# A long-convolution layer and a state-space layer in one kernel: queues in a list-scheduled order, x transposed by the DMA crossbar, and wide rotations

## The chip, the cores and the metric

One core of a Trainium2 chip. The metric is the device time of one execution in microseconds (us), as the median of several runs. Names of the engines: PE is TensorE (PEld its weight loads), DVE is VectorE, ACT is ScalarE, POOL is GpSimd, SP is SyncE, which here only issues DMA transfers; a "q" behind a name (SPq) is the engine's own instruction queue. A run is called slow when it lies over 1.5% above the fastest of its kernel; ratios use fast runs alone.

## The reference, cut to what matters

Two independent layers on 2048 x 1024 inputs in bf16, their outputs side by side.

```python
# A: k shifted (4 taps) times v, long convolution by FFT, gate by q
k_shift = sum over t of k_pad[:, t:t+S] * shift_k[:, 3-t]
kv = k_shift * v
y  = irfft(rfft(kv, 2S) * rfft(ssm_k, 2S))[:S] + kv * ssm_D
a  = q * y
# B: a diagonal complex state-space layer
Lam_bar = exp(dt * Lam);  B_bar = ((Lam_bar - 1) / Lam)[:, None] * Bmat
h_t = Lam_bar * h_{t-1} + B_bar @ x_t          # 2048 steps, 1024 complex states
b  = 2 * Re(h @ Cmat.T) + x * Dskip
out = concatenate([a, b], axis=-1)
```

Both kernels do layer A as a three-stage transform with matmuls: stage one (shift products on DVE, then matmuls, results to DRAM), stage two (load, matmul, product, halves swapped by DMA, matmul, back to DRAM) and stage three (load, matmul, product with q, store). Each stage needs all of the one before. Layer B runs in 16 chunks of 128 time steps. For each: U = B x on PE, a rotation by DVE that makes the recurrence real, two scans on DVE, a rotation back, y = C h on PE. The chunks follow one another through the scan's carry. Layer B has no dependency on layer A, so its U and y matmuls may fill whatever PE leaves free.

## The kernel before

Every chunk's x is loaded plain, transposed by PE and copied by ACT. The rotation is a list of products and sums of 1024 elements. It uses `u` as scratch, so the buffer of `u` is given back with the last operation (`state.pop`). [cuts are marked with ...]

```python
    def b_load_x(i):
        xn = xpool.tile([P, D], BF16, name="xn", bufs=3)
        dma(xn[:], x[i * T:(i + 1) * T, :])
        ...
    def b_xT(i, eng="s"):
        ...
        for dd in range(ND):
            nc.tensor.transpose(pt[:, dd, :], xn[:, dd * P:(dd + 1) * P], ident[:])
        ...
            nc.scalar.copy(xT[:], pt[:])

    def b_rot_ops(i):
        ...
        ops.append(lambda: nc.vector.tensor_mul(st["tb"][:], st["u"][:, 1, :, :], si[:]))
        ops.append(lambda: nc.vector.tensor_add(st["ta"][:], st["ta"][:], st["tb"][:]))
        ...
        ops.append(lambda: nc.vector.tensor_mul(st["u"][:, 1, :, :], st["tb"][:], eor[:]))
        def o14():
            nc.vector.tensor_add(st["h"][:, 1, :, :], st["h"][:, 1, :, :], st["u"][:, 1, :, :])
            state[("h", i)] = st["h"]
            state.pop(("u", i))
```

The order comes from a table of ticks, eight for each chunk. U of later chunks is spread over the ticks at a fixed rate, the three stages of layer A have fixed steps:

```python
    U_RATE1 = cfg.get("u_rate1", 1.5)
    U_RATE2 = cfg.get("u_rate2", 0.7)
    ...
    A1_STEP = cfg.get("a1_step", 2.0)
    A2_STEP = cfg.get("a2_step", 2)
    A3_STEP = cfg.get("a3_step", 1)
    ...
    for t_ in range(-1, NT):
        e = ev.get(t_, {})
        run(e.get("misc", []))
        run(interleave(e.get("pe_b", []), e.get("pe_a", [])))
        run(interleave(e.get("dve_b", []), e.get("dve_a", [])))
```

## Time and profile before

| | before |
|---|---|
| time, median of three runs | 434.61 us (430.33 to 434.89) |
| span of the profiled run | 431.1 us, granted clock 0.974 |
| PE / DVE / ACT busy | 380.7 / 350.7 / 303.6 us |

A busy PE is not a PE at its peak, so the tables of this document count "dense" PE work instead: the number of matmuls of each shape in a stretch times the time that one takes when they follow one another without a gap (0.056, 0.109 and 0.216 us for 128, 256 and 512 columns, the middle one an estimate from the others; the list below gives the same 128-column matmul a mean of 224 ns, since they overlap). What is missing to the length of the stretch is the loss.

The first fence is the table of busy time by stretch for the kernel before (length; then busy us and number of instructions of PE, PEld, DVE, ACT, POOL; granted clock, DMA share, GB/s):

```profile
0.00:180.00 180.00, 147.58 (x1753) 118.67 (x1754) 167.81 (x334) 143.01 (x239) 71.90 (x115) 0.96 0.74 242
180.00:431.10 251.10, 233.16 (x1964) 141.02 (x1961) 182.90 (x309) 160.56 (x292) 58.34 (x109) 0.98 0.71 234
```

From then on PE is busy 233 of 251 us; before it, 148 of 180. The second is the list by line for PE in the first 180 us (count, busy, mean ns, then idle time in front and what ended it):

```profile
L274 PE MATMUL pu<-xT,BT 128*128 128x128 bf16 x976 | 76.5, 224 | 0.5 <-ACT xT L263 0.3 <-ACT BT L605 0.2
L427 PE MATMUL psa<-acc,F1t 128*128 128x512 bf16 x64 | 24.6, 392 | 12.0 <-DVE acc L414 11.9
```

976 matmuls of U are 7.6 chunks. And 12 us of PE's idle time are spent in front of the stage-one matmul, waiting for the shift product on DVE; in this order U work that stands behind that matmul on PE is not begun meanwhile. The third is DVE's timeline:

```profile
171.24 0.67 DVE L414 TENSOR_TENSOR acc<-acc,vt 128x1024 bf16<-128x1024 bf16 x1
173.65 0.67 DVE L292 TENSOR_TENSOR ta<-u,ci 128x1024 bf16<-128x1024 bf16 x1
```

The last shift product ends at 171.9 us; the rotation of chunk 5 (the sixth, counted from 0) begins at 173.65.

### The profile page before, as it was taken

To read this page: it belongs to the slowest core of one execution; us is meant where nothing else is said; L and a number is where in the kernel's file an instruction comes from. 1 tells how busy PE (TensorE), PEld (TensorE's weight loads), DVE (VectorE), ACT (ScalarE), POOL (GpSimd) and SP (SyncE) were. 2 spreads that over 40 slices of the span, in tenths; PEclk is the share of its full clock that TensorE was granted. 3 is DMA by queue.
4 is the path that set the end of the run, shared out by engine and by line. 5 is a ranking of instruction groups with operands and counts; after the bars stand their busy time and mean duration, and the time that the engine had idled before them with its cause. 6 is when DMAs were issued, how large, how long until landed. Compare 5 with 4: busy or idle time off the path is not lost.

```text
span 431.1 us, 9757 instructions
## 1 busy us (share of the span) xinstructions
PE 380.7 (88%) x3713; PEld 259.7 (60%) x3713; DVE 350.7 (81%) x642; ACT 303.6 (70%) x531; POOL 130.2 (30%) x224
## 2 busy tenths in 40 slices
PE   2589799797987997999899999999899999997784
PEld 2578687575765875775556566566465666763331
DVE  2989999999999999936897979797959637976830
ACT  1977999787886887646678877878568783344451
POOL 4000344464654455311222232322122211012121
PEclk9979999999999899999999999999899999999989
DMA  7879987778776544397778687879666523959981
GB/s 247 285 255 309 336 289 254 265 240 249 276 235 205 167 163 159 120 334 238 229 241 263 217 247 245 265 234 295 195 217 181 165 69 135 298 176 396 403 316 73
DMA packets 41353, 102.23 MB, mean 237 GB/s; under 512 B 6621, under 2 KB 8925, under 8 KB 41306
## 3 DMA queue, kind: packets, MB, share of 16 engines
q1 hardware_dynamic: 27322, 58.60, 42.7%
q0 software_dynamic: 13984, 43.01, 28.8%
q8 instruction: 29, 0.48, 0.5%
q14 instruction: 18, 0.15, 0.1%
HBM read 59.64 MB, written 33.55 MB: 216 GB/s over the span
## 4 chain that ended last, share of the span: by engine, by line
PE 42%; DVE 28%; issue 12%; DMA 10%; ACT 5%; POOL 2%; SPq 0%; POOLq 0%; DVEq 0%; ACTq 0%
PE pu L274 13%; PE py L345 13%; DVE m L409 5%; PE psa L508 5%; DVE acc L410 4%; DMA hb<-ha 3%; PE psa L533 3%; PE psa L532 3%; DVE ta L305 2%; DVE tb L308 2%; DVE acc L414 2%; DMA out_dram<-ot 2%; POOL out_dram L88 2%; DMA bn<-in_B_C_re_dram 1%; PE pt L601 1%
## 5 line engine op out<-in xcount | busy, mean ns | idle before, releaser
L274 PE MATMUL pu<-xT,BT 128*128 128x128 bf16 x2048 | 156.1, 222 | 0.5 <-ACT xT L263 0.3
L274 PEld LDWEIGHTS <-BT 128*128 128x128 bf16 x2048 | 136.2, 100 | 33.5 <-issue 2.4
L345 PE MATMUL py<-CT,h 128*128 128x512 bf16 x512 | 140.2, 382 | 2.3 <-ACT yo L355 2.3
L345 PEld LDWEIGHTS <-h 128*128 128x128 bf16 x512 | 46.7, 98 | 45.5 <-issue 4.9
L88 POOL DMA_DIRECT2D hb<-ha x64 | 33.4, 526 | 88.9 <-ACT ha L509 85.0
L534 ACT CAST vsb<-psa 128x512 bf16<-128x512 f32 x64 | 37.0, 602 | 25.7 <-PE psa L533 24.8
L88 POOL DMA_DIRECT2D Ys_h<-ysbh x64 | 45.6, 716 | 30.8 <-ACT ysbh L475 29.4
L277 ACT CAST u<-pu 128x512 bf16<-128x512 f32 x64 | 39.4, 615 | 13.2 <-PE pu L274 13.1
L428 ACT CAST ysb<-psa 128x512 bf16<-128x512 f32 x64 | 38.5, 644 | 13.7 <-PE psa L427 13.3
L519 DVE TENSOR_TENSOR ha<-x,ha 128x1024 bf16<-128x1024 bf16 x32 | 21.9, 684 | 27.8 <-DMA hb<-ha 18.7
L475 ACT CAST ysbh<-psa 128x512 bf16<-128x512 f32 x64 | 38.7, 641 | 5.5 <-issue 2.3
L509 ACT CAST ha<-psa 128x512 bf16<-128x512 f32 x64 | 36.8, 598 | 7.3 <-PE psa L508 6.3
L509 ACT CAST x<-psa 128x512 bf16<-128x512 f32 x64 | 36.9, 593 | 7.3 <-PE psa L508 5.2
L308 DVE TENSOR_TENSOR_SCAN tb<-rtab,tb 128x1024 bf16<-128x1024 f32 x16 | 36.6, 2285 | 0.0
L305 DVE TENSOR_TENSOR_SCAN ta<-rtab,ta 128x1024 bf16<-128x1024 f32 x16 | 36.5, 2280 | 0.0
L427 PE MATMUL psa<-acc,F1t 128*128 128x512 bf16 x64 | 24.6, 392 | 12.0 <-DVE acc L414 11.9
L564 ACT CAST ot<-psa 128x512 bf16<-128x512 f32 x32 | 17.9, 589 | 24.4 <-DMA out_dram<-ot 14.8
L409 DVE TENSOR_TENSOR m<-krow,wbc 128x1024 bf16<-128x1024 bf16 x48 | 32.4, 675 | 0.0
L410 DVE TENSOR_TENSOR acc<-acc,m 128x1024 bf16<-128x1024 bf16 x48 | 32.3, 673 | 0.0
L532 PE MATMUL psa<-ha,wts 128*128 128x512 bf16 x64 | 24.5, 384 | 4.2 <-DVE ha L519 4.0
L88 POOL DMA_DIRECT2D Ys_kv<-ysb x32 | 17.8, 557 | 33.9 <-ACT ysb L428 33.9
L350 PE MATMUL py<-Dd,xT 128*128 128x128 bf16 x128 | 28.0, 219 | 0.0
(139 smaller groups left out, 628.5 us busy)
## 6 DMA issues: line engine op xcount, KB each, us to landing
Ys_kv<-ysb POOLq DMA_DIRECT2D x32, 256.0 KB, 2.9
Ys_h<-ysbh POOLq DMA_DIRECT2D x64, 128.0 KB, 3.3
l2k<-Ys_kv SPq DMA_DIRECT2D x16, 512.0 KB, 6.0
l2h<-Ys_h SPq DMA_DIRECT2D x16, 512.0 KB, 4.2
hb<-ha POOLq DMA_DIRECT2D x64, 128.0 KB, 3.7
Vs<-vsb POOLq DMA_DIRECT2D x16, 512.0 KB, 5.9
vv<-Vs SPq DMA_DIRECT2D x32, 256.0 KB, 6.6
xn<-in_B_x_dram SPq DMA_DIRECT2D x16, 256.0 KB, 4.3
```

Source lines behind the costliest of these rows:

```text
L88: return nc.gpsimd.dma_start(out_, in_)
L274: nc.tensor.matmul(pu[:, c, jl, :], BT[:, j, c, dd, :], xT[:, dd, :], start=(dd == 0), stop=(dd == ND - 1))
L277: nc.scalar.copy(u[:, :, j - 1:j + 1, :], pu[:])
L305: ops.append(lambda: nc.vector.tensor_tensor_scan(fl(st["ta"]), fl(rtab), fl(st["ta"]), 0.0, ALU.mult, ALU.add))
L308: nc.vector.tensor_tensor_scan(fl(st["tb"]), fl(rtab), fl(st["tb"]), 0.0, ALU.mult, ALU.add)
L345: nc.tensor.matmul(py[:], h[:, c, j, :], CT[:, j, c, dh * 512:(dh + 1) * 512], start=(j == 0 and c == 0), stop=(j == NJ - 1 and c == 1))
L409: ops.append(lambda jj=jj: nc.vector.tensor_mul(st["m"][:], krows[n2 - jj][:], wbc[:, jj, :]))
L410: ops.append(lambda: nc.vector.tensor_add(st["acc"][:], st["acc"][:], st["m"][:]))
L428: nc.scalar.copy(ysb[:, dh * 512:(dh + 1) * 512], pt[:])
L475: nc.scalar.copy(ysbh[:, :, n2l, :], pt[:].rearrange("p (c d) -> p c d", c=2))
L509: nc.scalar.copy(d_[:, dh * 512:(dh + 1) * 512], pt[:])
L532: nc.tensor.matmul(pt[:], wts[:, gi, 1, :], ha[:, dh * 512:(dh + 1) * 512], start=True, stop=False)
```

## The change

The intent: DVE and PE should not wait for one another. (1) Instead of tick tables, every piece of work is a task with a duration, dependencies, buffers and a priority; a small list scheduler in the kernel's source makes one fixed order of all queues from them. Parameters and phase tables have the first priority on every engine. (2) Transposes through PE use two PSUM banks. (3) Each rotation is two wide operations, a product of 4096 elements into a scratch tile and a sum of 2048. (4) x is loaded transposed by the DMA crossbar. The rewrite brings smaller changes with it: shift products and second-stage products are wide too, the first k and v loads go out on POOL's queue, and the filter taps are spread over the partitions by PE instead of by the DMA. The core of the diff (nearly the whole file is replaced; cuts marked with ...):

```diff
-    def b_load_x(i):
-        xn = xpool.tile([P, D], BF16, name="xn", bufs=3)
-        dma(xn[:], x[i * T:(i + 1) * T, :])
...
-            nc.tensor.transpose(pt[:, dd, :], xn[:, dd * P:(dd + 1) * P], ident[:])
...
+    def x_(i):
+        st["xT", i] = btile("xT", [P, ND, T])
+        nc.sync.dma_start_transpose(st["xT", i][:], x[i * T:(i + 1) * T, :])
...
-        ops.append(lambda: nc.vector.tensor_mul(st["tb"][:], st["u"][:, 1, :, :], si[:]))
-        ops.append(lambda: nc.vector.tensor_add(st["ta"][:], st["ta"][:], st["tb"][:]))
...
+    def rot_mul(i, src, Z):
+        st["m", i] = btile("mt", [P, 4, W], 1)
+        m = st["m", i][:].rearrange("p (a b) w -> p a (b w)", a=2)
+        s_ = src[:].rearrange("p b j t -> p (b j t)").unsqueeze(1).to_broadcast([P, 2, 2 * W])
+        nc.vector.tensor_mul(m, s_, win(Z))
+
+    E["r1"] = lambda i: rot_mul(i, st.pop(("u", i)), Z1)
...
-        run(interleave(e.get("pe_b", []), e.get("pe_a", [])))
-        run(interleave(e.get("dve_b", []), e.get("dve_a", [])))
...
+CFG = dict(PB=20.79, t0=31.9, lead=20.0, a1s=6.3, a1e=116.9, h_s=13.7, h_e=125.7, a2s=135.2, a2e=223.8, a3s=302.3,
+           a3e=340.0, u=5, xT=8, h=2, yo=2, ps_t=2, ps_u=2, ps_y=1, ps_a=3, kr=8, ld=5, acc=2, ysb=3, hk=3, hT=2, ysbh=2,
...
+    A(("tabA1",), "DVE", 4.1, [("dve3",)], [("u", 2), ("h", 2)], pr=-58)
...
+        A(("x", i), "SP", 1.5, acq=["xT"], pr=tu - c.get("xlead", 12.0) if i else -12, nbytes=int(256 * KB * 1.75))
+        for jp in range(4):
+            tj = tu + jp * c["PB"] / 8
+            A(("U", i, jp), "PE", 1.78, [("x", i)] + [("bc", 2 * jp + a, b) for a in (0, 1) for b in (0, 1)],
+              ["ps_u"] + (["u"] if jp == 0 else []), pr=tj, after=("U", i, jp - 1) if jp else None)
...
+    with tc.manual_schedule():
+        for t in make_plan(c).run():
+            E[t.name[0]](*t.name[1:])
```

In a task line, the first list holds what it depends on, the second the buffers that it takes, `pr` is its priority (lower is earlier). Both kernels have five buffers of `u`; the new one gives a buffer back with the first product of the rotation (`r1`).

## The prediction

> **What bounds the kernel now.** I read the page's first part, then the table of busy time by stage, the timeline and the chain of waits.
>
> ```profile
> PE 380.7 (88%) x3713; PEld 259.7 (60%) x3713; DVE 350.7 (81%) x642; ACT 303.6 (70%) x531; POOL 130.2 (30%) x224
> q1 hardware_dynamic: 27322, 58.60, 42.7%
> q0 software_dynamic: 13984, 43.01, 28.8%
> ```
>
> No engine is full over the span: TensorE (PE) is nearest, VectorE (DVE) next, the DMA engines near 72% (42.7 + 28.8). So I asked by stage. Columns: stretch, its length, busy time of each engine with instructions, granted clock, DMA share, GB/s.
>
> ```profile
> 0.00:44.00 44.00, 28.48 (x382) 25.97 (x383) 33.26 (x104) 29.53 (x47) 5.42 (x14) 0.92 0.85 276
> 44.00:180.00 136.00, 119.09 (x1375) 92.70 (x1373) 134.56 (x231) 113.49 (x193) 66.48 (x102) 0.97 0.70 231
> 180.00:390.00 210.00, 204.70 (x1840) 129.33 (x1837) 162.90 (x281) 144.50 (x262) 49.72 (x94) 0.99 0.70 222
> 390.00:431.10 41.10, 28.46 (x126) 11.68 (x124) 20.00 (x28) 16.06 (x30) 8.62 (x16) 0.94 0.76 293
> ```
>
> Four stages with different limits: a start in which no engine is full and DMA is busiest; 44 to 180 us (first stage of the convolution), where DVE is busy 134.56 of 136; 180 to 390, where PE is busy 204.70 of 210; a tail in which everything waits.
>
> A busy PE is not a PE at its peak, so I counted matmuls. The chain of waits (columns: start, length, what) shows the dense rates:
>
> ```profile
> 178.40 1.79 PE pu L274 x32
> 180.19 0.86 PE py L345 x4
> ```
>
> 32 matmuls of 128 columns in 1.79 us are 56 ns each, 4 of 512 in 0.86 us are 215. From the list by line and shape: 2688 matmuls of 128 columns (2048 for pu, 128 each for the skip term and for transposes of B, C, x and the filter) are 150 us, 896 of 512 columns are 193, 128 of 256 columns at about 109 ns (half the 512 rate plus overhead, an estimate) are 14. Dense PE work is **357 us** of 431; some 74 us are idle, slow-clock or stalled. The same count in the four stages gives about 22, 111, 201 and 25 us: losses of 22, 25, 9 and 16. That is what a better order can win; the 357 it cannot, except by removing matmuls.
>
> The tail, in the chain:
>
> ```profile
> 398.12 2.90 issue
> 401.01 0.02 POOLq L88
> 401.03 0.54 POOL out_dram L88
> 401.57 2.38 issue
> ```
>
> POOL issues an output store every 2 to 3 us; the page's slices of GB/s stand near 400 there. The third convolution stage moves 4 x 4.2 MB (two halves of Vs, q, output), and most of it runs after the scan chain has nothing left to hide it with.
>
> **What the Trainium skill says.** (1) "TensorE: Matmul & The Clock Gate", section "Wait — 56ns, not 53.3ns?": warm start-to-start is 55.6 ns at 128 columns, 215.7 at 512. The trace agrees (56 and 215), so PE cannot go faster per matmul. (2) "VectorE: DVE Perf Modes", "The perf-mode tier table": tensor_tensor on bf16 reaches 2x only, 1224 ns for 2048 elements. A wider op therefore saves a fixed cost and no element time. The timeline agrees on size: 1024-element products start every 0.60 us (0.53 of it is 1024 elements at two per cycle of 0.96 GHz). (3) "Advanced Engine Details and Errata", "X-Bar Transpose (TRN2)": transpose DMAs are as fast as regular ones; "DMA: Bandwidth & Descriptors", "Latency and other measured facts", gives 261 GB/s for a non-contiguous case. No run here shows one yet. (4) The same DMA page, "Issuing engines are not separate DMA queues": all queues share 16 engines, so moving early k and v loads to POOL's queue saves issue time, not bandwidth.
>
> **The change, part by part.**
>
> Rotations. Before, per chunk, 12 products and sums of 1024 elements, 2 scans of 2.20 us and six small carry ops. The timeline shows how well they are packed already:
>
> ```profile
> 58.01 0.67 DVE L410 TENSOR_TENSOR acc<-acc,m 128x1024 bf16<-128x1024 bf16 x1
> 58.61 0.67 DVE L328 TENSOR_TENSOR u<-tb,eor 128x1024 bf16<-128x1024 bf16 x1
> 59.21 0.67 DVE L414 TENSOR_TENSOR acc<-acc,vt 128x1024 bf16<-128x1024 bf16 x1
> ```
>
> The mean of 0.67 overlaps the next; the cost is 0.60. So a chunk is 12 x 0.60 + 4.4 + about 0.6 = 12.2 us. After: two products of 4096 (2.13 + 0.07 = 2.20 each), two sums of 2048 (1.07 + 0.07, and 0.07 because each now waits on its forerunner), scans 4.4, three small ops 0.5: about 11.7. Gain 0.5 x 16 = **8 us of DVE**, far less than the drop from 14 wide instructions to 6 suggests. Shift products: 8 x 0.60 = 4.8 before, 2.20 + 1.2 + 2 x 0.67 = 4.7 after: 1 to 2 us in all. Second-stage product: 1.14 for 1.20, 2 us over 32. Four B evacuations, the x copy and two table casts leave DVE: 4.5 us; smaller parameter ops, 3. DVE falls from 351 to about **330 us**.
>
> x by crossbar. Removes 128 PE transposes, 128 x 0.056 = 7.1 us, and on ScalarE (ACT) 15 copies of 1.06, 15.9 us. It also frees two PSUM tiles for the other transposes (the pool keeps two banks). Filter broadcast through PE adds 8 x 0.22 = 1.7. PE work becomes 357 - 7 + 2 = **352 us**. ACT: -15.9, +4 B copies, +4.3 table copies, about +1 for the broadcast: 297.
>
> Order. The instruction order shows the parameter chain and tables first on each engine; all shift products done during chunks 0 to 4, second stage in chunks 5 to 13, third stage in 13 to 15, with only five q products after the last rotation. So the DMA-heavy third stage moves beside PE work, and shift products begin before the B matrices are all in.
>
> Sum by stage. DVE leads until the shift products end: about 20 us of tables and parameters + 16 x 4.7 + 5 x 11.7 = 154 us, beginning near 9 (parameters land at 7.3, and copy and Exp follow), and some 7 us of gaps: 170 us, where before needed about 180 and had DVE idle 11 us in the first 44. PE has by then done its share, some 140 us of 352 (132 before by 180). Left: 212 us of PE; at the 96% density of 180 to 390 before, 220. Then the tail: after the last rotation eight y groups (about 6.9 us of PE, part of it already in the 212), last evacuation and a store landing in 3 to 4 us, little of it hidden: +4. Span 170 + 220 + 4 = 394 at most of the old inefficiency; with the order somewhat tighter in the middle (98%), 389. The times exceed the span by 3.5 us (434.6 against 431.1). I choose **394 us**, 9% less.
>
> **Rivals.** (a) DVE becomes the bound throughout: 330 us plus a start of 9 and a tail of 11 is 350, below PE's sum, unless the stride-0 broadcast and overlapping windows of the wide products cost the 2x mode. Then 48 products of 4096 take 2.1 us longer each, +102, DVE passes 430, and the time is 440 or more. For it: no such pattern is in this trace. Against: innermost runs are dense bf16. 3%. (b) Transfers become the wait. 72% of 431 is 308 us of DMA; with slower x transposes (I add 10) and 1 MB less of broadcast, about 316 in 390, 81%; in the second stage 37 MB plus x and y in some 130 us are 300 GB/s, and the table showed 222 to 276 at shares of 0.70 to 0.85. Waits for swapped halves (18.7 us of DVE idle before) could grow: time 405 to 415. For it: a fixed order blocks a whole queue behind a late load. 20%. (c) A fixed order made from planned durations meets real ones; PE, DVE and ACT drift and stall each other as before: 410 to 425. 10%. (d) The order fits well, PE is dense from 25 us to the end: 376 to 382. 20%.
>
> **Range and chances.** The sum gives 389 to 397; (d) takes it to 378, (b) to 411. Eight in ten: 378 to 411. "Same" needs over 426, meaning all the tail's and start's gain lost: 4%. Slower only through (a) or a badly slow transpose: 2%. Faster: 94%.
>
> **What would show it.** Right: the dense count 352 us and losses of 35 to 45 instead of 74; over half of the gain in the start and tail; the last stage under 12 us behind the last rotation; DVE busy near 330 with 4096-wide products starting every 2.2 us; no x copy on ACT; second-stage DMA share above 0.8. Wrong: 4096-wide products near 4.3 us (a); x transposes landing in over 10 us or holding the SP queue, so that first pu matmuls start after 25 us (b); long waits of PE and ACT for one another with every engine under 85% (c).

## The result, and the profile after

405.76 us (403.26 to 409.58, four runs) against 433.83 (430.33 to 434.89) for the kernel before in the same rounds. A ratio here is always the mean time of one kernel's fast runs over that of the other's of the same rounds, so not quite the ratio of these medians: 0.935, 95% interval 0.928 to 0.941. Faster, by 6.5%; 12 us slower than predicted, inside the range. The profiled run took 403.26 us, with a span of 401.5. First the page's totals and the hardware DMA queue (packets, MB, share of the 16 engines' time), then the table by stretch:

```profile
PE 366.2 (91%) x3593; PEld 248.6 (62%) x3593; DVE 336.4 (84%) x338; ACT 291.6 (73%) x527; POOL 132.1 (33%) x228
q1 hardware_dynamic: 40864, 57.17, 47.3%
```

```profile
0.00:44.00 44.00, 31.06 (x382) 26.49 (x383) 30.32 (x83) 34.55 (x61) 12.15 (x26) 1.00 0.99 265
44.00:165.00 121.00, 117.08 (x1487) 95.48 (x1485) 113.02 (x98) 105.99 (x180) 59.42 (x89) 1.00 0.74 245
165.00:190.00 25.00, 19.90 (x186) 12.60 (x184) 24.34 (x21) 10.29 (x20) 3.92 (x8) 0.94 0.71 232
190.00:380.00 190.00, 183.01 (x1468) 107.28 (x1467) 159.34 (x129) 133.07 (x254) 51.70 (x97) 1.00 0.81 261
```

DVE lost 304 instructions but only 14 us. The start is no fuller than it was (PE 31 of 44 us), and there is a new hole: from 165 to 190 us, where stage two has to begin, PE is busy 19.9 of 25. The cut at 180 us, and PE's U work in the first 180:

```profile
0.00:180.00 180.00, 161.75 (x2025) 131.97 (x2025) 157.95 (x193) 148.06 (x254) 74.44 (x120) 1.00 0.79 243
180.00:401.50 221.50, 204.44 (x1569) 116.67 (x1568) 178.43 (x146) 143.55 (x273) 57.61 (x108) 0.99 0.79 259
```

```profile
L588 PE MATMUL ps_u<-xT,BT 128*128 128x128 bf16 x1280 | 79.2, 221 | 0.1
L698 PE MATMUL ps_a<-acc,F1t 128*128 128x512 bf16 x64 | 20.3, 379 | 0.6 <-DVE acc L691 0.3 <-ACT ysbh L750 0.3
```

The stretch after 180 us shrank from 251.1 to 221.5 us. Since the cut lies at the same time in both kernels, this is the whole gain of 29.6 us in span by construction. 1280 matmuls of U are exactly ten chunks, against 7.6; the wait for shift products in front of the stage-one matmul fell from 12.0 to 0.6 us. But DVE is not further on at that time:

```profile
168.27 0.69 DVE L691 TENSOR_TENSOR acc<-acc,ld 128x1024 bf16<-128x1024 bf16 x1
168.88 2.29 DVE L600 TENSOR_TENSOR mt<-u,Z 128x4096 bf16<-128x4096 bf16 x1
181.15 2.29 DVE L600 TENSOR_TENSOR mt<-u,Z 128x4096 bf16<-128x4096 bf16 x1
```

The last shift product ends at 169.0 (before: 171.9), and the rotation of chunk 5 begins at 181.15, which is 7.5 us *later* than before. So at 180 us five chunks are rotated or nearly so in both kernels (before, the sixth rotation is half done); after the change PE has U ready for five more, before for two and a half. Dense PE work by the count described above:

| | dense to 180 us | dense left | length of the rest | dense share of the rest |
|---|---|---|---|---|
| before | 132.4 | 225.6 | 251.1 | 0.90 |
| after | 152.1 | 200.5 | 221.5 | 0.91 |

Of the 25.1 us less that are left at 180 us, 5.4 are work that the change removed (358.0 us in all before, 352.6 after), 19.7 were done earlier, and 17 of these are U (304 matmuls of 0.056 us). The rest is worked off at nearly the same density, as the sum of two things that cancel in part: a better tail, and a new hole at its beginning.

Losses by stage, before: 22 (to 44 us), 25 (to 180), 9 (to 390), 16 (tail). After: 20 (to 44), 8 (to 172), 5 (172 to 190), 9 (to 380), 7 (tail from 380). Stage one with the passage to stage two gained 12 us, the tail 10, the start 2, the removed work 5.4.

One rival is the clock: the profiled runs were granted 0.974 before and 0.992 after, and within the fast runs of one kernel a lower clock goes with a longer time (0.992 and 403.26 us, 0.979 and 407.62 us for the changed kernel). It carries little of the gain. At nearly equal clocks, 0.978 for the kernel before (430.99 to 433.46 us in runs of the rounds below) and 0.979 for the changed one (407.62), 23 to 26 us remain of the 28.

What was left undone stands in the timeline of SP's queue (start, length of the issuing, what):

```profile
16.24 6.27 SPq L576 DMA_TRANSPOSE xT<-in_B_x_dram  x2
...
25.09 2.83 SPq L576 DMA_TRANSPOSE xT<-in_B_x_dram  x1
...
28.60 1.23 SPq L576 DMA_TRANSPOSE xT<-in_B_x_dram  x1
...
30.49 1.23 SPq L576 DMA_TRANSPOSE xT<-in_B_x_dram  x1
...
45.29 0.38 SPq L558 DMA_DIRECT2D ld<-in_B_B_im_dram  x1
```

Six crossbar loads of x between 16 and 32 us, three of them for chunks 5 to 7, which cannot be used before a buffer of `u` comes free at the first rotation, sit between the loads of B (issued at 24.51, 28.02, 29.93 and so on); the last B load is issued at 45.3. Every rotation needs all of B. And DVE waits for v, whose load is behind them too:

```profile
44.15 0.69 DVE L691 TENSOR_TENSOR acc<-acc,ld 128x1024 bf16<-128x1024 bf16 x1 [6.68 <-DMA ld<-in_A_v_dram]
...
56.14 2.29 DVE L600 TENSOR_TENSOR mt<-u,Z 128x4096 bf16<-128x4096 bf16 x1 [0.94 <-ACT u L590]
```

The first rotation begins at 56.14 us. Before, the first line of a rotation stood almost 19 us earlier:

```profile
37.31 0.68 DVE L292 TENSOR_TENSOR ta<-u,ci 128x1024 bf16<-128x1024 bf16 x1
```

### The profile page after: what moved, and what is told of

Its sections match the earlier page's. It is cut to its first block, busy times and chain, and to the rows that moved or that the text cites. A ratio compares the mean times of both kernels' runs of the same rounds, so it can differ in the third digit from the quotient of the medians.

```text
span 401.5 us, 9098 instructions
## 1 busy us (share of the span) xinstructions
PE 366.2 (91%) x3593; PEld 248.6 (62%) x3593; DVE 336.4 (84%) x338; ACT 291.6 (73%) x527; POOL 132.1 (33%) x228
## 4 chain that ended last, share of the span: by engine, by line
PE 42%; DMA 15%; issue 14%; DVE 13%; ACT 9%; POOL 4%; SPq 2%; POOLq 0%; ACTq 0%; DVEq 0%
PE ps_y L641 14%; PE ps_u L588 12%; PE ps_a L805 5%; PE ps_a L772 5%; DMA wts<-a_c_W 4%; DMA hab<-hab 3%; DVE h L618 3%; DMA Ys_kv<-ysb 3%; DVE hab L796 2%; DMA Ys_h<-ysbh 2%; DMA ld<-in_B_B_re_dram 2%; ACT ysbh L750 2%; POOL out_dram L850 2%; PE ps_a L698 1%; POOL Ys_h L757 1%
## 5 line engine op out<-in xcount | busy, mean ns | idle before, releaser
L641 PE MATMUL ps_y<-CT,h 128*128 128x512 bf16 x512 | 138.1, 381 | 3.6 <-ACT yo L656 1.6
L588 PE MATMUL ps_u<-xT,BT 128*128 128x128 bf16 x2048 | 126.0, 221 | 0.1
L618 DVE TENSOR_TENSOR_SCAN h<-rtab,h 128x1024 bf16<-128x1024 f32 x32 | 71.5, 2276 | 0.3
L590 ACT CAST u<-ps_u 128x512 bf16<-128x512 f32 x64 | 37.9, 604 | 41.9 <-PE ps_u L588 41.8
L796 DVE TENSOR_TENSOR hab<-x,hab 128x2048 bf16<-128x2048 bf16 x32 | 38.5, 1221 | 14.8 <-ACT hab L779 6.5
L600 DVE TENSOR_TENSOR mt<-u,Z 128x4096 bf16<-128x4096 bf16 x16 | 36.6, 2289 | 11.2 <-ACT u L590 11.0
L779 ACT CAST hab<-ps_a 128x512 bf16<-128x512 f32 x64 | 36.2, 600 | 10.8 <-DMA l2h<-Ys_h 5.7
L785 ACT CAST x<-ps_a 128x512 bf16<-128x512 f32 x64 | 36.9, 599 | 5.2 <-PE ps_a L772 5.0
L750 ACT CAST ysbh<-ps_a 128x512 bf16<-128x512 f32 x64 | 36.8, 637 | 4.3 <-DMA Ys_h<-ysbh 2.6
L600 DVE TENSOR_TENSOR mt<-h,Z 128x4096 bf16<-128x4096 bf16 x16 | 36.5, 2283 | 0.0
L553 PE MATMUL ps_t<-ident,ld 128*128 128x128 bf16 x256 | 21.1, 233 | 9.2 <-DMA ld<-in_B_B_re_dram 5.8
```

What stands on the lines that cost most here:

```text
L588: nc.tensor.matmul(pu[:, w, jl, :], BT[:, 2 * jp + jl, w, d, :], xT[:, d, :], start=(d == 0), stop=(d == ND - 1))
L590: E["ue"] = lambda i, jp: nc.scalar.copy(st["u", i][:, :, 2 * jp:2 * jp + 2, :], st.pop(("pu", i, jp))[:])
L600: nc.vector.tensor_mul(m, s_, win(Z))
L618: nc.vector.tensor_tensor_scan(gf[:, a * W:(a + 1) * W], rt1, gf[:, a * W:(a + 1) * W], 0.0, ALU.mult, ALU.add)
L641: nc.tensor.matmul(py[:], h[:, 1 - w, j, :], CT[:, j, w, dh * 512:(dh + 1) * 512], start=(j == 0 and w == 0), stop=(j == NJ - 1 and w == 1))
L750: nc.scalar.copy(st["yh", qd, n4, w // 2][:, :, w % 2, :], st.pop(("pa", qd, n4, w))[:].rearrange("p (c d) -> p c d", c=2))
```

## The experiments

All outputs are right. Before each run its author wrote down an "own theory" and at least one "rival", another explanation with another number. "Before" had medians of 433.13, 433.20, 432.44 and 432.50 us in the rounds beside these runs. Twelve kernels ran. In nine of their traces 37 to 51 of some 3600 PE records are missing, so counts and busy times of PE are a little low there; the runs with the work put back, with three chunks ahead, and the last one are complete.

### x through PE again, in the new order

The crossbar load is replaced by a plain load, eight transposes and a copy on ACT; buffers had to move for it (x 8 to 7, k rows 8 to 7), and the list was planned anew.

```diff
-        A(("x", i), "SP", 1.5, acq=["xT"], pr=tu - c.get("xlead", 12.0) if i else -12, nbytes=int(256 * KB * 1.75))
+        A(("xl", i), "SP", 1.5, acq=["xn"], pr=tu - c.get("xlead", 12.0) if i else -12, nbytes=256 * KB)
+        A(("xt", i), "PE", .45, [("xl", i)], ["ps_t", "xT"], ["xn"], pr=tu - 2 if i else -12)
+        A(("x", i), "ACT", .91, [("xt", i)], [], ["ps_t"], pr=tu - 2 if i else -12)
```

> The new kernel with x transposed on the tensor engine again (128 transposes, 16 copies on ACT; order planned anew, x buffers 7 and 2 in the same memory, key ring 7 in place of 8). My theory, dense PE work plus losses: PE work rises by 7 us, ACT by 16; most of the 7 and a little more shows: about 415 us, ratio to the kernel before 0.955. Rival A, the freed transpose banks and ACT time are the main gain: 0.975 or more. Rival B, a crossbar transpose costs the transfers what it saves the engines: 0.935, no change from the new kernel.

Measured: 424.0 us (421.87 to 426.81), ratio 0.981 (0.974 to 0.988). That looks like 18 us for the crossbar, but the trace of this kernel has one line that spoils the experiment:

```profile
55.22 0.69 DVE L702 TENSOR_TENSOR acc<-acc,ld 128x1024 bf16<-128x1024 bf16 x1 [23.39 <-DMA ld<-in_A_v_dram]
```

The new plan had put the first load of v far back, DVE stood idle for 23.39 us at once, and the first rotation moved from 56 to 72 us, which would be enough for nearly all of the 18. This run does not say what the crossbar is worth.

### The crossbar alone, in the old order

```diff
-        xn = xpool.tile([P, D], BF16, name="xn", bufs=3)
-        dma(xn[:], x[i * T:(i + 1) * T, :])
+        xT = xpool.tile([P, ND, T], BF16, name="xT", bufs=XT_BUFS + 3)
+        nc.sync.dma_start_transpose(xT[:], x[i * T:(i + 1) * T, :])
```

> The kernel before with x by crossbar DMA alone (same tick order, 10 x buffers in the memory of 7 and 3). My theory: PE work falls by 7 us, but the first stage there is bound by DVE, so only part shows: 427 to 430 us, ratio 0.985. Rival A (banks and ACT are the main gain): 0.96. Rival B (transposes as dear as they save): 1.00.

Measured: 433.92 us, ratio 1.001 (0.991 to 1.010): the number of rival B, not of the own theory. PE's busy time fell from 380.7 to 371.0 (49 of its 3585 records are missing) and ACT's from 303.6 to 288.4; the time did not move. The interval leaves room for some 4 us either way.

### The removed work put back as idle work, in the new order

Since the first of these runs was spoilt, the same question was asked in a form that leaves the new order and its loads alone: the first eight matmuls of each chunk's U done twice, and each x tile copied onto itself by ACT.

```diff
+        if jp == 0:
+            for d in range(ND):
+                nc.tensor.matmul(pu[:, 0, 0, :], BT[:, 0, 0, d, :], xT[:, d, :], start=(d == 0), stop=(d == ND - 1))
...
+        E["xc"] = lambda i: nc.scalar.copy(st["xT", i][:], st["xT", i][:])
```

> The changed kernel in its own order, with the engine work that the crossbar had removed put back as idle work: the first 8 matmuls of each chunk's U are done twice (128 matmuls of 128 columns, 7.1 us of dense TensorE work) and ScalarE copies each x tile onto itself (16 copies of 1.06 us). The loads stay on the crossbar. Own theory (from the second stage on TensorE sets the time, in the first it has slack): half of the doubled work and more lies in chunks whose U is done ahead in the first 180 us; the 6 chunks left cost 6 x 8 x 56 ns = 2.7 us, and the whole is 2 to 5 us, ratio 0.939 to 0.947. Rival one (the removed work is worth all of its 7 us): ratio 0.951 or more. Rival two (worth nothing, as in the kernel before): 0.933 to 0.937.

Measured: 409.1 us (407.36 to 410.41), ratio 0.945 (0.938 to 0.951): 3 to 4 us slower than the changed kernel, in the range of the own theory. The intervals of the two ratios overlap, so "worth a few us" is supported, "worth all of 7" is less so, and "nothing" is not excluded by much. Nor does the trace show the own theory's mechanism. The idle work delayed the start as well:

```profile
60.86 2.29 DVE L603 TENSOR_TENSOR mt<-u,Z 128x4096 bf16<-128x4096 bf16 x1 [2.27 <-ACT u L593]
```

That is the first rotation, 4.7 us later than in the changed kernel; chunk 5 follows at 188.50 instead of 181.15, and 1152 matmuls of U are done by 180 us instead of 1280. How much of the 3 to 4 us is this start, and how much is work in the full second stage, is open.

### Rotations as narrow operations, same order

```diff
-        nc.vector.tensor_mul(m, s_, win(Z))
+        for a in range(2):
+            for b in range(2):
+                nc.vector.tensor_mul(st["m", i][:, 2 * a + b, :], s_[:, b, :], z_[:, a + b, :])
```

(and the sums likewise in two of 1024)

> The new kernel with each rotation product as four products of 1024 and each sum as two of 1024, same order, same result. My theory: 12 instructions of 0.60 in place of 2 x 2.20 + 2 x 1.2 is about 0.5 us more per chunk, DVE +8 us of which a part is hidden: 408 to 411 us, ratio 0.943. Rival: the wide products are what made DVE leave the path: ratio 0.96 or more. A third, independent narrow products overlap the waits of one another: no change, 0.935.

Measured: 403.85 us (403.13 to 404.12), ratio 0.934 (0.928 to 0.940), the same as the changed kernel's 0.935 within some 3 us. DVE's timeline of this run, to be read beside the line at 168.88 us of the changed kernel above:

```profile
252.03 2.50 DVE L602 TENSOR_TENSOR mt<-u,Z 128x1024 bf16<-128x1024 bf16 x4
```

Four narrow products take 2.50 us, one wide one 2.29: 0.07 us for each operation saved (0.21 / 3). Over the kernel DVE's busy time gains 7.4 us (343.8 to 336.4) and the kernel's time nothing. From one rotation's start to the next, where DVE does nothing else, it is less: 12.27 us wide (168.88 to 181.15) and 12.57 narrow (170.42 to 182.99), since the sum behind a wide product waits for its end. Widening the operations is worth nothing here. What both kernels of this comparison keep, against the kernel before, is the scratch tile that lets `u` go after the first product.

### The third stage moved beside the last rotations, in the old order

```diff
-    A2_STEP = cfg.get("a2_step", 2)
-    A3_STEP = cfg.get("a3_step", 1)
+    A2_STEP = cfg.get("a2_step", 1.6)
+    A3_STEP = cfg.get("a3_step", 1.25)
```

> The kernel before with its second stage at 1.6 ticks a group in place of 2 and the third at 1.25 in place of 1, so the third stage lies beside the last rotations; nothing else. My theory: the tail's loss of 16 us falls to about 8, ratio 0.98 (425 us). Rival: the second stage is held by its transfers and cannot go faster, and the crowding costs PE waits there: ratio 1.00 or more.

Measured: 426.45 us (424.86 to 428.12), ratio 0.986 (0.980 to 0.993): 6.7 us, near what was expected. The trace agrees on the place: the last rotation ends at 409.65 us (410.03 before), and what follows it takes 13.5 us instead of 21.1. This is the tail's part of the gain, had in the old kernel by two numbers.

### Table part of the chain late, in the new order

```diff
-    A(("tabA1",), "DVE", 4.1, [("dve3",)], [("u", 2), ("h", 2)], pr=-58)
-    A(("eo",), "ACT", 4.8, [("sin1",), ("sin2",), ("par_rest",)], pr=-55)
+    A(("tabA1",), "DVE", 4.1, [("dve3",)], [("u", 2), ("h", 2)], pr=10)
+    A(("eo",), "ACT", 4.8, [("sin1",), ("sin2",), ("par_rest",)], pr=10)
```

(and nine more tasks of the chain in the same way)

> The changed kernel with the table part of the parameter chain (phase tables, sines, the products of Z2) no longer first: on VectorE and ScalarE the first shift products, the copies of B and of the first results stand ahead of it. Own theory: the first rotation at 56.14 us waits for results of the last B loads, not for tables, which are finished at 29.6 us; putting them 5 to 8 us later changes the start by at most 3 us, ratio 0.934 to 0.942. Rival (the table chain first is what the new order gains at the start): the first rotation moves out by 5 to 8 us and the time with it, ratio 0.947 to 0.953.

Measured: 412.42 us (411.97 to 414.26), ratio 0.953 (0.947 to 0.958). The own theory falls: it allowed 3 us, it was 6.7, the size that the rival named. The theory had looked only at when the tables are needed. DVE's waits in the first 90 us of this kernel:

```profile
DVE acc L691 <- DMA ld<-in_A_v_dram: 8.8, 2, 5.1
DVE BT L564 <- PE ps_t L553: 6.4, 3, 3.6
```

In the changed kernel the same waits are 7.2 and 4.1. The first rotation moves to 60.30 us, 4.2 later. The tables are some 13 us of DVE and 11 of ACT by the list's planned durations; put later, they stand in the queues between the copies of B, and a B load can start only when such a copy has freed its buffer. That this chain makes the 4.2 us is a reading, and the trace supports it only in part: the last B load is issued at 45.67 instead of 45.29 us, the loads of v at 41.95 and 46.93 instead of 40.03 and 45.77. In the first 44 us DVE was as busy as before (30.41 us against 30.32), and the granted clock was 0.88 instead of 1.00, which no run separates from the order.

### Loads of x for chunks 5 to 7 after the loads of B

```diff
-        A(("x", i), "SP", 1.5, acq=["xT"], pr=...
+        A(("x", i), "SP", 1.5, [("bl", 7, 1)] if 5 <= i < 8 else [("x", i - 1)] if i >= 8 else [], acq=["xT"], pr=...
```

> The changed kernel with one thing moved: the crossbar loads of x for chunks 5 to 7 go after the last load of B instead of between the B loads (and those of later chunks after them, as before). Own theory: in the changed kernel VectorE leads the first stage, and its first 56 us lose because seven crossbar loads at 16 to 31 us (1.23 us of the sync queue each, two of them 6.27) stand in front of the loads of B and v; then the first rotation should come at 50 to 52 us instead of 56.14, the 6.68 us wait for v at 44.15 should shrink below 3, and the time fall by 4 to 5 us, ratio to the kernel before 0.924. Rival (only the sum of TensorE's work and its gaps in the second stage count; the start is hidden): first rotation earlier, time unchanged at 0.933 to 0.936.

Measured: 396.97 us (396.19 to 398.54), ratio 0.916 (0.910 to 0.922). Twice the expected gain. (The loads at 16 to 31 us are six in the trace, not seven.) The last B load is issued at 37.3 us instead of 45.3, the wait for v is 4.44 instead of 6.68 us, the first rotation begins at 50.42 instead of 56.14:

```profile
37.32 0.47 SPq L558 DMA_DIRECT2D ld<-in_B_B_im_dram  x1
...
42.27 1.33 SPq L576 DMA_TRANSPOSE xT<-in_B_x_dram  x1
```

```profile
165.00:190.00 25.00, 24.79 (x299) 19.13 (x301) 24.38 (x19) 12.21 (x22) 6.52 (x11) 1.00 0.74 239
```

About 5 us were expected, and the first rotation shows 5.7; the rest lies in the second fence: the hole at the passage to stage two is gone (PE busy 24.79 of 25, was 19.90). A reading that fits, not tested by itself: with the rotations some 5.7 us earlier (chunk 5 begins at 175.49 instead of 181.15), a buffer of `u` is free and U work is at hand while stage two waits for its first loads.

### Loads of x for chunks 8 to 15 later in the queue

```diff
+        A(("x", i), "SP", 1.5, [("r1", i - 6)] if i >= 8 else [], acq=["xT"], pr=...
```

> The changed kernel with the crossbar loads of chunks 8 to 15 put later in the sync queue: each after the start of the rotation of the chunk six before it, by when its buffer has long been free. Own theory: in the second stage the sync queue stands for up to 11 us at an x load whose buffer is not free, and the loads for stage two of the convolution behind it come late (weights landing 10.91 us after issue order at 249); with x later these waits on the x line fall from 42.0 + 22.8 us to under 15 in sum, TensorE's gaps between 180 and 300 us shrink, time falls 4 to 6 us, ratio 0.922. Rival (the loads themselves are slow because DMA is near full in that stretch, or TensorE is held by the small order drift and not by the queue): waits move to another line of the queue, time unchanged, 0.932 to 0.937.

Measured: 402.55 us (401.70 to 403.64), ratio 0.929 (0.924 to 0.935): 3.2 us by the medians, less than expected, and the interval overlaps that of the changed kernel (0.928 to 0.941), so a gain is likely and not certain. What SP's queue waited for at the x line (L576) and the stage-two loads (L766): first the changed kernel, then this one (us, times, longest).

```profile
SPq L766 <- PE ps_a L772: 49.6, 8, 11.0
SPq L576 <- PE ps_a L698: 42.0, 2, 26.3
...
SPq L576 <- PE ps_a L772: 22.8, 2, 11.5
```

```profile
SPq L766 <- PE ps_a L772: 57.0, 10, 9.7
...
SPq L576 <- PE ps_a L698: 17.9, 1, 17.9
SPq L576 <- PE ps_a L772: 11.4, 3, 4.6
```

The waits at the x line fell from 64.8 to 29.3 us in these rows, not below 15; the waits for the stage's own buffers stay, and one for the end of stage one moved to another line, as the rival had it (L764 for `Ys_kv`, 4.1 before, 30.1 now). Standing behind an x load is a small part of it.

### Both moves of the x loads

> Both moves of x loads together: chunks 5 to 7 after the last B load, chunks 8 to 15 after the rotation six chunks before. Own theory: the two gains lie in different stages, so they add: 8 to 11 us under the changed kernel, ratio 0.912. Rival (the stages share one bound, a gain at the start is given back where TensorE is full): no more than the better of the two alone, 0.922 or above.

Measured: 395.59 us (394.68 to 401.06), ratio 0.912 (0.906 to 0.919). The profiled run was a slow one, so its trace is not used. This is 10 us under the changed kernel, in the own theory's range of 8 to 11. But it is not to be told from the first move alone (0.916), so that the two gains add is not shown.

### TensorE held to three chunks ahead

```diff
-            A(("U", i, jp), "PE", 1.78, [("x", i)] + [("bc", ...
+            A(("U", i, jp), "PE", 1.78, [("x", i), ("r1", i - 3) if i > 2 else None] + [("bc", ...
```

> The changed kernel with one more dependency in its list: the products U of chunk i may not start before the rotation of chunk i - 3 has begun, so TensorE may be at most three chunks ahead of VectorE instead of five. Own theory: the gain of the first stage is that TensorE, which has slack there, does U work of later chunks ahead: at 180 us the changed kernel had done 1280 of these matmuls with 5 rotations begun, the kernel before 976 with 5 begun. Held to three ahead, 2 chunks x 128 x 56 ns = 14 us of dense work fall back into the second stage, where TensorE is full: the time rises by 12 to 17 us, to 418 to 423, ratio 0.963 to 0.975, and the matmuls of U done by 180 us fall to about 1020. Rival (the gain is from packing VectorE and from the third stage beside the last rotations; the U work finds room anyhow): no more than 4 us, ratio below 0.945.

Measured: 418.56 us (414.06 to 423.10), ratio 0.963 (0.956 to 0.971), 12.8 us by the medians, in the expected range; the rival allowed 4. The cut at 180 us and the count of U:

```profile
0.00:180.00 180.00, 153.25 (x1769) 117.59 (x1769) 158.30 (x193) 144.52 (x247) 74.15 (x120) 0.98 0.79 248
180.00:415.40 235.40, 218.98 (x1824) 131.78 (x1824) 178.51 (x146) 146.61 (x280) 57.48 (x108) 0.98 0.74 240
```

```profile
L588 PE MATMUL ps_u<-xT,BT 128*128 128x128 bf16 x1024 | 62.7, 221 | 0.0
```

DVE did the same work by 180 us (158.30 against 157.95), the rotation of chunk 5 began at the same time (181.24 against 181.15); PE did two chunks less (1024 against 1280 matmuls). Dense work to 180 us is 137.8, left 214.8 in 235.4 us, a share of 0.91 again. One line of the list differs, and DVE's side shows no other effect of it; the order of the rest was planned anew around it, and the granted clock of the first 180 us was 0.98 instead of 1.00. Note also what is left: with 1024 matmuls of U by 180 us this kernel is hardly further ahead than the kernel before (976), and still 14 us faster than it. Running ahead is about half of the gain, not all of it.

### Six chunks ahead

On top of both moves of the x loads; the room comes from one x buffer and one k row.

```diff
-           a3e=340.0, u=5, xT=8, h=2, ... kr=8, ...
+           a3e=340.0, u=6, xT=7, h=2, ... kr=7, ...
```

> The version with both moves of the x loads, with six buffers for u in place of five, so that TensorE may be six chunks ahead of VectorE; the room comes from one x buffer (8 to 7) and one row buffer of k (8 to 7). Own theory (work that TensorE does before about 180 us is taken out of the full second stage): held to three ahead the time rose by 13 us for two chunks; one chunk more can give at most 128 x 56 ns = 7.2 us, but the first stage of this version has only some 10 us of TensorE gaps left, and the order must find room for it: 3 to 6 us under 395.6, 390 to 393, ratio 0.900 to 0.908. Rival (the first stage is as full as it gets; fewer buffers of x and k take back what the sixth buffer gives): 394 to 398, ratio 0.911 to 0.919.

Measured: 394.14 us (392.37 to 398.45), ratio 0.915 (0.910 to 0.920), against 0.912 with five buffers: the rival. 1312 matmuls of U by 180 us are only a quarter of a chunk more than ten. The first stage has little room left: PE's loss between 172 and 190 us is below 1 us in this trace, and 8 of 128 in the stretch before it.

### B loads before the first loads of k, with both moves

```diff
-b_p=1.5,
+b_p=-5.0,
```

> The version with both moves of the x loads and, besides, the B loads ahead of the first loads of k (priority -5 instead of 1.5 in the list). Own theory: the x moves gave 10 us; the B loads earlier should bring the first rotation no later than 52 us and leave the end at 393 to 397, ratio 0.908 to 0.916. Rival (B earlier takes the DMA from k and v, on which VectorE's first products wait): 398 to 402, ratio 0.92 to 0.93.

Measured: 405.47 us (400.71 to 437.20; the 437 is the profiled run, at a clock of 0.852), ratio 0.934 (0.929 to 0.940). A miss: ten us lost against both moves alone. The rival's size is nearer, though beyond its upper edge; since the only trace is of a slow run, what B displaced was not settled.

The version to keep is the changed kernel with its x loads moved: 395.6 to 397.0 us, against 405.8 and 433.2.

## Why the prediction was right or wrong

**Right in size and direction.** 405.76 lies in the range, 12 us above the 394.

**Dense work of 352 us: right.** Counted 352.6. DVE 336.4 for "near 330", ACT 291.6 for 297.

**"Gain 0.5 x 16 = 8 us of DVE" for the wide operations: right only against narrow ones in the same order** (7.4 us of busy time). A rotation takes 12.27 us after the change, by the prediction's own sum 12.2 before and 11.7 after, so against the old kernel there was no gain of this kind; and none in the kernel's time. Rival (a) did not come: 4096-wide products take 2.29 us, not 4.3.

**"x by crossbar. Removes 128 PE transposes, 128 x 0.056 = 7.1 us": right as work**; putting it back cost 3 to 4 us of time in the new order, of which the later start may be a good part, and taking it out was not measurably worth anything in the old.

**"Losses of 35 to 45": 49. "Over half of the gain in the start and tail": wrong.** They gave 12 of 29.6 us. The start gave 2: the tables come early, but the first rotation does not. The larger part is the first stage. "The last stage under 12 us behind the last rotation": 15.5 (from 386.0 to 401.5 us), also missed.

**"170 us, where before needed about 180": the first half right by luck, the comparison wrong.** The shift products end at 169.0. But the sum that gave 170 counts five rotations of 11.7 us, shift products of 4.7 and 16 us of gaps; the trace has four finished rotations of 12.3, shift products of 5.0 (50.13 to 55.1) and 22 us of gaps (DVE busy 147 of 169), and these errors cancel. Before, the shift products had ended at 171.9. DVE's side of the first stage gained 3 us, not 10. The gain that the sum needed came from the clause beside it, "PE has by then done its share, some 140 us of 352 (132 before by 180)": by 180 us PE had done 152.1. The prediction wrote this down as a by-product and did not say that it *was* the mechanism; the run held to three chunks shows that it is the largest single part of it.

**The step that failed: "Left: 212 us of PE; at the 96% density of 180 to 390 before, 220. Then the tail: ... +4".** At 172 us 208 us were left, and they took 229.5, a density of 0.91. 190 to 380 us did reach 0.95, nearly as assumed. What the sum lacked was the passage from stage one to stage two: a loss of 5 us in 18. By 180 us PE had done just the ten chunks of U that five buffers allow; the waits that the trace names there are 2.6 us for the first stage-two weights (`wts`), 1.4 for ACT and 1.1 for DVE. And the tail lost 7 us, not 4. The span of 394 would be 397.5 as a time, by the prediction's own 3.5; the chosen 394 leaned on "somewhat tighter in the middle (98%)", which did not come.

**Rival (b), "Transfers become the wait", with "x transposes landing in over 10 us or holding the SP queue, so that first pu matmuls start after 25 us" as its mark.** The mark did not show: U began at 19.64 us and x transposes landed in 4.5 us. Yet the time of this rival, 405 to 415, is what was measured, and its reason, "a fixed order blocks a whole queue behind a late load", is near what happened: the queue was held. It hit the later B loads and v, not the first U. Moving three x loads behind the loads of B gave back 8.8 us, the better part of the 12 that were missed. The mark was set at the first matmul, when the first rotation was what mattered. Rivals (c), 410 to 425, and (d), 376 to 382, did not come.

**Where the gain is from**, each by its own run, sizes that need not add up: PE two chunks further ahead, 12.8 us; tables first, 6.7; third stage beside the last rotations, 6.7 (in the old kernel); work removed by the crossbar, 3 to 4 at most of it (the start moved too); wide operations, 0; given away by the place of the x loads, 8.8. Why the old order did not run further ahead was not tested by itself: its list paces U, its PE queue stood 12 us in front of stage-one matmuls, and its rotation holds `u` to the end; any of these could do it.

## What to carry to other kernels

When one engine leads a stage and another is full in the next, count how much of the second engine's work is done when the first stage ends; here nearly every us of it done early came off the end, until the stage was full (five chunks ahead gave 13 us over three, for 14 us of work; six gave nothing over five). In a fixed order, a load that is not needed soon must not stand in front of one that is: the scheduler that finds a buffer free will put it there. And an instruction saved on an engine that is not the bound, or made wider, is worth what the next stage can use of it, which here was little or nothing. An experiment that puts work back can also move the start: look at the first rotation before the difference is put down to the work.

## What the Trainium skill lacked or had wrong

- "DMA: Bandwidth & Descriptors", section "Issuing engines are not separate DMA queues", calls the sequencer's time to start a DMA usually small beside the DMA. For crossbar loads it was not: 1.23 us of SP's queue for one load at the least, where plain loads mostly took 0.33 to 0.53 and the load itself landed in 4.5. (The 6.27 us for two in a row are not the crossbar's alone: three plain loads of k took 4.99 from 9.44 us on; the DMA share of the first 44 us is 0.99.) With the bytes that they put on the engines, three such loads in the wrong place cost 8.8 us.
- "Advanced Engine Details and Errata", section "X-Bar Transpose (TRN2)", says that they are as fast as regular DMAs. Landing was slower in each pair of one order: 5.6 us against 4.3 for 256 KB in the old order (medians), 4.5 against 2.8 in the new. Its next lines expect about 90% of a plain copy's bandwidth, which is nearer. What that section lacks is the packets that go with it: with the crossbar alone added, those under 512 B rose from 6621 to 23262, and the hardware queue took 45.7% of 429.5 us for the same 58.60 MB, where it had 42.7% of 431.1, 7% more engine time.
- "VectorE: DVE Perf Modes", section "The TRN2 errata — SBUF-src ops pay a fixed extra latency per instruction", names two fixed costs, 58 cycles in its table and about 150 measured on single operations. Between operations in a row the runs show 0.07 us each (2.50 us for four of 1024 against 2.29 for one of 4096), near the smaller one (60 ns), 0.30 us for the eight operations saved in a whole rotation (12.57 against 12.27), and none of it in the kernel's time.
- No page gives the cost of order itself. That the issuing queue is what waits is stated; what it costs is not: a queue that stands at a transfer whose buffer is not free (SP at an x load in stage two, 11.5 us at the longest) keeps all transfers behind it back, though they could go.
